# Reordering the start of a four-layer attention and MLP kernel on one Trainium2 core

## The chip, the cores and the metric

The kernel runs on one core of one Trainium2 chip. The metric is the device time of one execution in microseconds (us), and the number that counts is the median over runs. The engines are TensorE (PE in the profile, with its weight loads as PEld), VectorE (DVE), ScalarE (ACT), GpSimd (POOL) and SyncE (SP), which does nothing here but issue DMA transfers.

## The reference, cut to what matters

```python
x = A_x                                            # 1 x 2048 x 512, bf16
x = x + attention(layernorm(x), wqkv, w_phi, wo)   # layer 0
x = x + mlp(layernorm(x), W_gate, W_up, W_down)    # layer 1
x = x + attention(layernorm(x), ...)               # layer 2, the same weights
x = x + mlp(layernorm(x), ...)                     # layer 3, the same weights

def attention(x):                                  # 32 heads of 16
    q, k, v = split(x @ wqkv)
    phi(u) = concat(softmax(u @ w_phi), softmax(-u @ w_phi))
    kv = phi(k).T @ v                              # sums over all 2048 rows
    z = phi(k).sum(rows)
    return (phi(q) @ kv) / (phi(q) @ z + 1e-6) @ wo

def mlp(x):
    return (relu(x @ W_gate) * (x @ W_up)) @ W_down    # 512 -> 1376 -> 512
```

## The kernel before

The 2048 rows are 16 tiles `t` of 128 rows, which lie in `x_sb` from the start to the end. Every step of the whole program is recorded as an operation with an engine, a function, the data that it reads and writes, and two guessed costs in nanoseconds (`ii`, the time its engine is held; `lat`, the time until its result is there). A list scheduler (`Program.schedule`) then plays the program through eight times with these guesses and with a guess for DMA (`DMA_ISSUE`, `DMA_FIXED`, `DMA_BW`), and keeps the best order. So each engine runs a fixed order of instructions, and each instruction waits for semaphores of what it reads. A changed guess or priority can change the order on any engine.

What the first 55 us do:

- **Constants on VectorE.** `rowi` is a row 0..31, made by doubling (L446, L449); a 32x32 transpose (L450) gives `coli`, `colf` (L452) is its first column as f32, and four comparisons (L456) give the identity `ident`. From it come `m8` (L458) and `mask2` (L459). GpSimd clears small buffers (`vones` L463, `hr0` L465) and copies the mask (`kvsm` L466).
- **The folded key weights.** The 16x16 maps `w_phi` are folded into the key and query weights. `wk0` to `wk3` (L494) are four blocks of the key weights. TensorE transposes each (`WkT mm`, L527), ACT or DVE copies the result out (`WkT cp`, L532 and L534), a product with the block diagonal `BD` (L518, from `w128` and `m8`) makes `Wkp` (`Wkp mm` L542, `Wkp cp` L546 and L548). No key tile can start before all four blocks of `Wkp` are there. The query weights take the same way, transposed by DMA (`wT`, L485).
- **The tiles.** For every tile `t`: statistics `stat` (L559) and `aggr` on DVE, the reciprocal deviation `ln` and `rstd` (L562, L564) on ACT, the normalized tile `y` on DVE (L579) or, for the tiles in `POOL_Y`, on GpSimd (`nmr` L574, `yp` L576). Its transpose `yT` is made by TensorE and ACT for tiles 0, 1 and 2 (L588, L591) and by a DMA transpose on SP (L594) for the others. Then TensorE makes the keys `K` (L612) and the values `V` (L635), four matmuls of 128x512 each; ACT takes the exponentials (L617), DVE sums and normalizes them (L618, L626), and `kv` (L671) sums over the tiles. The queries (L651) and the attention per tile follow.

All loads go over two queues. SP issues, in this order, `wk0`..`wk3`, the tiles `x2`-`x3`, `wv`, `x4`-`x7`, the four `wT`, `x8`-`x11`, `x12`-`x15`, then the transposes `yT0.3`, `yT0.4` and so on to `yT0.15` (the name is layer, then tile), then the weights of the later layers. ACT issues `x0`, `wphi` (the load of `w128`, in elements of 32 bytes) and `x1`. Five matmuls of 128x512 on zeros (`warm`, L514) run on TensorE before the first weights land.

Of the kernel before, what the change touches and what calls it, by code (L numbers as in the profile page):

```python
# [5 lines left out]
FP32 = mybir.dt.float32  # L6
BF16 = mybir.dt.bfloat16
ALU = mybir.AluOpType
ACT = mybir.ActivationFunctionType
AX = mybir.AxisListType  # L10
# [38 lines left out]

class Program:  # L50
    SYNC = 40.0
    DMA_ISSUE, DMA_FIXED, DMA_BW = 520.0, 1500.0, 230.0
    TR_ISSUE, TR_FIXED, TR_TIME = 1250.0, 1050.0, 250.0

    def __init__(self, n_dma_sems=64):
        self.ops = []
        self.n_dma_sems = n_dma_sems

    def op(self, eng, fn, reads=(), writes=(), parts=(), ii=100.0, lat=None, name="", claims=(), after=(), dma=None, nbytes=0):
# [37 lines left out]
        self.ops.append(o)  # L97
        return o


    def links(self):
        for o in self.ops:
# [26 lines left out]
    def forward(self, prio, look=60.0):  # L129
# [4 lines left out]
        for o in ops:  # L134
            o.npend = len(o.deps) + len(o.order)
            o.ready = 0.0
            o.prio = prio[o.i]
            for t in o.tiles:
                tiles[id(t)] = t
        for t in tiles.values():  # L140
            t.slot, t.before, t.left = None, (), len(t.users)
            t.pool.held = [None] * len(t.pool.slots)
        free = dict.fromkeys(ENGINES, 0.0)
        bus = 0.0
        ready = {e: [] for e in ENGINES}
        for o in ops:
# [231 lines left out]
def build_kernel(nc, A_x, A_wqkv, A_w_phi, A_wo, B_x, B_W_gate, B_W_up, B_W_down, out):  # L378
# [20 lines left out]
    BD = sb("BD", [NC, 128])  # L399
    w128 = sb("w128", [NC, 16])  # L400
    m8 = sb("m8", [8])
    rowi, coli, colf = sb("rowi", [32]), sb("coli", [32]), sb("colf", [1], FP32)
    ident = sb("ident", [128])
    mask2 = sb("mask2", [8])
    eps = sb("eps", [1], FP32)
# [35 lines left out]
    c_BD = [res("BD", a) for a in range(4)]  # L441
    c_row, c_col = res("row"), res("col")
    wm, c_warm = tile(p_ga, "warm")
    op("dve", lambda e: e.memset(wm.ap(), 0.0), writes=[c_warm], ii=150, lat=210, name="warm")
    op("dve", lambda e: e.memset(ident[:], 0.0), writes=[c_id], ii=60, lat=100, name="id0")
    op("dve", lambda e: e.memset(rowi[:, 0:1], 0.0), writes=[c_row], ii=30, lat=70, name="row0")  # L446
    for k in range(5):
        n = 1 << k
        op("dve", lambda e, n=n: e.tensor_scalar(rowi[:, n:2 * n], rowi[:, 0:n], float(n), None, ALU.add), reads=[c_row], writes=[c_row], ii=70, lat=150, name="row")  # L449
    op("dve", lambda e: e.transpose(coli[:], rowi[:]), reads=[c_row], writes=[c_col], ii=100, lat=215, name="col")  # L450
    c_colf = res("colf")
    op("dve", lambda e: e.tensor_copy(colf[:], coli[:, 0:1]), reads=[c_col], writes=[c_colf], ii=70, lat=150, name="colf")  # L452
    c_idq = [res("identq", q) for q in range(4)]
    for q in range(4):
        sl = slice(32 * q, 32 * q + 32)
        op("dve", lambda e, sl=sl: e.tensor_scalar(ident[sl, sl], rowi[sl, :], colf[sl, :], None, ALU.is_equal), reads=[c_row, c_colf, c_id], writes=[c_idq[q]], ii=75, lat=150, name="identq")  # L456
    c_id = c_idq
    op("dve", lambda e: e.tensor_reduce(m8[:], ident[:].rearrange("p (h d) -> p h d", d=16), AX.X, ALU.add), reads=c_id, writes=[c_m8], ii=200, lat=290, name="m8")  # L458
    op("dve", lambda e: e.tensor_reduce(mask2[:].rearrange("p (a b) -> p a b", b=2), ident[:].rearrange("p (a f b) -> p a b f", f=16, b=2), AX.X, ALU.add), reads=c_id, writes=[c_m2], ii=200, lat=290, name="mask2")  # L459
    op("dve", lambda e: e.memset(eps[:], 1e-5), writes=[c_eps], ii=35, lat=70, name="eps")  # L460
    va_all = p_va.slots
    for i in range(16):
        op("pool", lambda e, i=i: e.memset(va_all[i][:, :, 128:130], 1.0), writes=[res("va1", i)], ii=60, name="vones")  # L463
    for i in range(2):
        op("pool", lambda e, i=i: e.memset(p_hr.slots[i], 0.0), writes=[res("hr0", i)], ii=500, name="hr0")  # L465
    op("pool", lambda e: e.tensor_copy(kvs[:, :, 136:144], mask2[:].unsqueeze(1).to_broadcast([P, 8, 8])), reads=[c_m2], writes=[res("kvsm")], ii=200, lat=280, name="kvsm")  # L466


    xv = A_x.rearrange("b (t p) d -> p (b t) d", p=P)
    outv = out.rearrange("b (t p) d -> p (b t) d", p=P)  # L470
# [19 lines left out]
    for ic in range(4):  # L490
        t, r = tile(p_hT, "wkn", ic)
        wk_n.append((t, r))
    def load_wk(ic):
        load("sp", lambda e: e.dma_start(wk_n[ic][0].ap(), A_wqkv[ic * 128:(ic + 1) * 128, 512:1024]), [wk_n[ic][1]], 131072, f"wk{ic}")  # L494
    load_x("act", 0, 1)
    load_wk(0)
    load("act", lambda e: e.dma_start(w128[:], A_w_phi.rearrange("(c h) d f -> (h d) c f", c=4)), [c_w128], 16384, "wphi")
    load_wk(1)
    load_wk(2)
    load_x("act", 1, 2)  # L500
    load_wk(3)
    load_x("sp", 2, 4)
    c_wv, c_wo = res("wv"), res("wo")
    load("sp", lambda e: e.dma_start(wv[:], A_wqkv[:, 1024:1536].rearrange("(c p) f -> p c f", p=P)), [c_wv], 524288, "wv")
    load_x("sp", 4, 8)
    for ic in range(4):
        load_wT(t_wq, c_wqT, 0, ic)
    load_x("sp", 8, 12)
    load_x("sp", 12, 16)


    pt_w, r_w = tile(p_ps, "warm")
    for k in range(5):
        op("pe", lambda e: e.matmul(pt_w.ap(), wm.ap()[:, 0:128], wm.ap(), start=True, stop=True), reads=[c_warm], writes=[r_w], ii=430, lat=600, name="warm")  # L514


    for a in range(4):
        op("dve", lambda e, a=a: e.tensor_tensor(BD[:].rearrange("p c (a f b) -> p c a f b", f=16, b=2)[:, :, a], w128[:].unsqueeze(3).to_broadcast([P, 4, 16, 2]),  # L518
                                                 m8[:, 2 * a:2 * a + 2].unsqueeze(1).unsqueeze(1).to_broadcast([P, 4, 16, 2]), ALU.mult),
           reads=[c_w128, c_m8], writes=[c_BD[a]], ii=190, lat=280, name="BD")  # L520

    for ic in range(4):
        pt, pres = tile(p_ps, "WkT", ic)
# [32 lines left out]
    def ln(l, ts):  # L556
# [9 lines left out]
        for t in ts:  # L566
            s = t // 4
            if (l, s) not in yT:
                yT[l, s] = Tile(f"yT{l}.{s}", p_yT)
            dst = yT[l, s]  # L570
            rr = res("yT", l, t, tile=dst)
            yt, yr = tile(p_y, "y", l, t)
            if (l, t) in POOL_Y:
                op("pool", lambda e, t=t: e.tensor_scalar(nmr[:, t, :], mv[:, t, 0:1], rstd[:, t, :], -1.0, ALU.mult, ALU.mult), reads=[res("mv", t), res("rstd", t)], writes=[res("nmr", t)],  # L574
                   ii=100, lat=170, name=f"nmr{l}.{t}")
                op("pool", lambda e, t=t, yt=yt: e.tensor_scalar(yt.ap(), x_sb[:, t, :], rstd[:, t, :], nmr[:, t, :], ALU.mult, ALU.add), reads=[res("x", t), res("nmr", t), res("rstd", t)],  # L576
                   writes=[yr], claims=[dst], ii=1000, lat=1050, name=f"yp{l}.{t}")
            else:
              op("dve", lambda e, t=t, yt=yt: e.tensor_scalar(yt.ap(), x_sb[:, t, :], mv[:, t, 0:1], rstd[:, t, :], ALU.subtract, ALU.mult),  # L579
               reads=[res("x", t), res("mv", t), res("rstd", t)], writes=[yr], claims=[dst], ii=323, lat=405, name=f"y{l}.{t}")  # L580
            c = (t % 4) * 128
            if (l, t) in PE_Y:
                pt, pres = tile(p_ps, "yps", l, t)

                def mm(e, yt=yt, pt=pt):
                    b16 = pt.ap().bitcast(BF16)
                    for k in range(4):
                        i = e.transpose(b16[:, k * 128:(k + 1) * 128], yt.ap()[:, k * 128:(k + 1) * 128], ident[:])  # L588
                    return i
                op("pe", mm, reads=[yr] + c_id, writes=[pres], ii=230, lat=400, name=f"yT{l}.{t}")  # L590
                op("act", lambda e, pt=pt, dst=dst, c=c: e.activation(dst.ap()[:, :, c:c + 128], pt.ap().bitcast(BF16)[:, 0:512].rearrange("p (k n) -> p k n", k=4), ACT.Copy),  # L591
                   reads=[pres], writes=[rr], ii=477, lat=600, name=f"yTcp{l}.{t}")
            else:
                op("sp", lambda e, yt=yt, dst=dst, c=c: e.dma_start_transpose(dst.ap()[:, :, c:c + 128], yt.ap()), reads=[yr], writes=[rr],  # L594
                   dma="tr", nbytes=131072, name=f"yT{l}.{t}")
# [277 lines left out]
    for l in (0, 2):  # L873
        for s in range(NS):
            for c in range(4):
                q_chunk(l, s, c)
        kv_sums(l)
        for t in range(NT):
            attn_tile(l, t)
            ln(l + 1, [t])  # L880
        for s in range(NS):
            hv = [(0, 2), (2, 4)] if s == 0 else [(0, 4)]
            halves_of[l + 1, s] = hv
            glu_slab(l + 1, s, hv)
            for t in range(4 * s, 4 * s + 4):
                down(l + 1, t, last=(l == 2))
                if l == 0:
                    ln(2, [t])
                    kv_tile(2, t)
    pr.schedule(ROUNDS)  # L890
    pr.prepare()
    block = E(nc.Block())
# [15 lines left out]

ROUNDS = 8
ACT_RZ = {(0, t) for t in range(16)} | {(2, t) for t in range(0, 16, 2)}  # L910
POOL_Y = {(0, t) for t in range(4, 16)}
PE_Y = {(0, 0), (0, 1), (0, 2), (1, 0), (1, 1), (2, 15), (3, 0), (3, 1)}
PE_O = {(0, 0), (0, 1), (2, 0), (2, 1)}

# [42 lines left out]
```

## Time and profile before

| | |
|---|---|
| median of 8 runs | 398.33 us |
| lowest and highest run | 397.07 and 399.66 us |
| the profiled execution's own time | 398.31 us |
| its span, first to last instruction | 396.5 us |
| TensorE busy | 380.3 us, 96% of the span |
| VectorE, ScalarE, GpSimd busy | 71%, 50%, 11% |
| mean granted TensorE clock | 0.994 |

The span leaves out 1.8 us of the measured time that lie around the instructions. "L612" is line 612 of the kernel before. In a timeline row the first number is the start in us, the second the time that the row's instructions took together, `x4` their count, and the bracket the idle time of the engine before them with what ended it.

### The profile page before, as it was taken

How to read it: one execution, taken by the hardware profiler on the slowest of the kernel's cores; microseconds unless marked ns; L12 is line 12 of the kernel's file. 1: busy time of each engine (PE TensorE's matmuls, PEld its weight loads, DVE VectorE, ACT ScalarE, POOL GpSimd, SP SyncE). 2: the span in 40 equal slices, each digit the busy share in tenths (PEclk: the TensorE clock that was granted, in tenths of full speed). 3: DMA queues.
4: the chain of work that ended last, by engine and by line, in shares of the span. 5: the costliest groups of instructions: out<-in, count | busy, mean ns of one | idle time of the engine just before them, and what ended most of it. 6: DMA issues, size and time to landing. Idle time of an engine off the chain costs nothing.

```text
span 396.5 us, 6502 instructions
## 1 busy us (share of the span) xinstructions
PE 380.3 (96%) x2362; PEld 209.6 (53%) x2405; DVE 283.5 (71%) x599; ACT 199.7 (50%) x615; POOL 43.4 (11%) x143
## 2 busy tenths in 40 slices
PE   6879999899999999999999999989999999999996
PEld 3434755677655444444444466567765544444442
DVE  8969957998889636536699993799888962433424
ACT  4969779765444304303149966976544430303300
POOL 2371012221111000000000001222111100000000
PEclk9989999999999999999999999999999999999999
DMA  8846900134231402002022000014423140110012
GB/s 224 176 94 154 354 30 8 34 76 85 45 63 28 80 15 40 14 2 40 13 43 52 2 2 2 13 32 78 80 50 61 26 79 15 40 37 17 0 48 73
DMA packets 63439, 23.02 MB, mean 58 GB/s; under 512 B 54352, under 2 KB 63408, under 8 KB 63408
## 3 DMA queue, kind: packets, MB, share of 16 engines
q1 hardware_dynamic: 62592, 22.33, 24.7%
q8 instruction: 19, 0.31, 0.3%
q10 hardware_dynamic: 816, 0.28, 0.3%
q14 instruction: 12, 0.10, 0.1%
HBM read 7.91 MB, written 2.10 MB: 25 GB/s over the span
## 4 chain that ended last, share of the span: by engine, by line
PE 74%; ACT 12%; DVE 8%; DMA 2%; POOL 2%; issue 1%; SPq 0%
PE pb L794 30%; PE pb L846 17%; PE pb L635 6%; ACT expq L655 5%; PE pb L612 4%; PE pb L764 4%; PE pb L671 4%; ACT phik L617 3%; PE pb L651 2%; PE pb L822 2%; PE pb L848 2%; PE pb L704 2%; DVE t L738 1%; DVE stats L559 1%; DVE hT L802 1%; ACT sm L718 1%
## 5 line engine op out<-in xcount | busy, mean ns | idle before, releaser
L801 ACT ACTIVATE gate<-pb 128x512 bf16<-128x512 f32 (+1 forms) x100 | 50.7, 509 | 101.3 <-PE pb L794 100.5
L794 PE MATMUL pb<-yT,Wg 128*128 128x512 bf16 (+1 forms) x395 | 83.0, 336 | 0.3
L794 PE MATMUL pb<-yT,Wu 128*128 128x512 bf16 (+1 forms) x393 | 82.5, 336 | 0.4
L802 DVE TENSOR_TENSOR hT<-gate,pb 128x512 bf16<-128x512 bf16 (+1 forms) x100 | 56.4, 576 | 35.6 <-PE pb L794 35.2
L846 PE MATMUL pb<-Wd,hT 128*128 128x512 bf16 x310 | 73.6, 379 | 0.4
L794 PEld LDWEIGHTS pb<-yT,Wg 128*128 128x128 bf16 x400 | 37.7, 98 | 32.9 <-DVE hT L802 1.5
L794 PEld LDWEIGHTS pb<-yT,Wu 128*128 128x128 bf16 x400 | 38.4, 98 | 28.0 <-DVE hT L802 0.5
L846 PEld LDWEIGHTS pb<-Wd,hT 128*128 128x128 bf16 x320 | 31.2, 98 | 37.9
L852 DVE TENSOR_TENSOR x_sb<-x_sb,pb 128x512 bf16<-128x512 bf16 x32 | 21.8, 682 | 37.3 <-PE pb L848 37.3
L559 DVE BATCH_NORM_STATS2 stats<-x_sb 128x6 f32<-128x512 bf16 x64 | 43.1, 685 | 0.4
L618 DVE TENSOR_REDUCE z<-phik 128x64 f32<-128x1024 bf16 x32 | 37.5, 1208 | 3.7 <-ACT rz L623 3.7
L655 ACT ACTIVATE expq<-pb 128x512 bf16<-128x512 f32 x64 | 35.0, 608 | 8.7 <-PE pb L651 8.7
L738 DVE TENSOR_TENSOR t<-pb,sm 128x384 bf16<-128x384 f32 x64 | 32.6, 549 | 7.6 <-POOL sm L729 6.8
L617 ACT ACTIVATE phik<-pb 128x512 bf16<-128x512 f32 x64 | 35.6, 641 | 4.6 <-PE pb L612 4.5
L562 ACT ACTIVATE lnv<-mv,eps 128x1 f32<-128x1 f32 (+2 forms) x56 | 16.4, 298 | 41.4 <-DVE mv L560 41.3
L725 POOL TENSOR_TENSOR sm<-sm 128x64 f32<-128x64 f32 x32 | 10.5, 327 | 228.3 <-ACT sm L718 228.3
L612 PE MATMUL pb<-Wkp,yT 128*128 128x512 bf16 x124 | 30.8, 391 | 2.7 <-DMA yT<-y 2.5
L767 DVE TENSOR_TENSOR x_sb<-x_sb,pb 128x512 bf16<-128x512 bf16 x32 | 21.7, 679 | 14.2 <-PE pb L764 14.2
L764 PE MATMUL pb<-wo,oT 128*128 128x512 bf16 x120 | 30.5, 379 | 0.7
L651 PE MATMUL pb<-yT,Wqp 128*128 128x512 bf16 x122 | 29.7, 380 | 1.3 <-DVE t L738 0.8
L635 PE MATMUL pb<-wv,yT 128*128 128x512 bf16 x125 | 30.2, 383 | 0.2
L579 DVE TENSOR_SCALAR y<-x_sb,mv,rstd 128x512 bf16<-128x512 bf16 x52 | 21.1, 409 | 3.3 <-ACT rstd L564 3.3
(69 smaller groups left out, 384.8 us busy)
## 6 DMA issues: line engine op xcount, KB each, us to landing
out_dram<-x_sb SPq DMA_DIRECT2D x16, 128.0 KB, 1.7
x_sb<-in_A_x_dram SPq DMA_DIRECT2D x3, 512.0 KB, 5.3
Wg<-in_B_W_gate_dram SPq DMA_DIRECT2D x2, 640.0 KB, 7.9
Wu<-in_B_W_up_dram SPq DMA_DIRECT2D x2, 640.0 KB, 9.1
Wd<-in_B_W_down_dram SPq DMA_DIRECT2D x1, 1280.0 KB, 13.3
yT<-y SPq DMA_TRANSPOSE x56, 2.5
hT<-in_A_wqkv_dram SPq DMA_DIRECT2D x4, 128.0 KB, 3.8
wv<-in_A_wqkv_dram SPq DMA_DIRECT2D x1, 512.0 KB, 6.2
```

Of the source, the lines that this page charges most:

```text
L559: op("dve", lambda e, t=t: e.bn_stats(stats[:, t, :], x_sb[:, t, :]), reads=[res("x", t)], writes=[res("st", t)], ii=600, lat=690, name=f" ...
L612: i = e.matmul(kt.ap(), src.ap()[:, ic, c0:c0 + 128], Wkp[:, ic, :], start=(ic == 0), stop=(ic == 3))
L617: op("act", lambda e, s=s: e.activation(ft.ap()[:, s, :], kt.ap(), ACT.Exp, scale=(1.0, -1.0)[s]), reads=[kr], writes=[fr2[s]], ii=477, la ...
L618: op("dve", lambda e: e.tensor_reduce(zt.ap().rearrange("p (a b) -> p a b", b=2), ft.ap().rearrange("p s (a f b) -> p (s a) b f", f=16, b= ...
L635: i = e.matmul(vt.ap(), src.ap()[:, ic, c0:c0 + 128], wv[:, ic, :], start=(ic == 0), stop=(ic == 3))
L651: i = e.matmul(qt.ap(), Wqp[:, ic, c * 128:(c + 1) * 128], src.ap()[:, ic, :], start=(ic == 0), stop=(ic == 3))
L655: op("act", lambda e, g=g: e.activation(es[g][0].ap(), qt.ap(), ACT.Exp, scale=(1.0, -1.0)[g]), reads=[qr], writes=[es[g][1]], ii=477, lat ...
L764: i = e.matmul(wt.ap(), oT_.ap()[:, c, :], wo[:, c, :], start=(c == 0), stop=(c == 3))
L794: i = e.matmul(pt.ap()[:, 0:n], W[:, ic, fc * 128:(fc + 1) * 128], src.ap()[:, ic, a * 128:b * 128], start=(ic == 0), stop=(ic == 3))
L801: op("act", lambda e: e.activation(st_.ap()[:, 0:n], gt.ap()[:, 0:n], ACT.Relu), reads=[gr], writes=[sr], ii=110 + n * .72, lat=230 + n * ...
L802: op("dve", lambda e: e.tensor_tensor(ht.ap()[:, a * 128:b * 128], st_.ap()[:, 0:n], ut.ap()[:, 0:n], ALU.mult), reads=[sr, ur], writes=[h ...
L846: i = e.matmul(pt.ap(), hT[l, s, fc].ap()[:, c:c + 128], Wd[:, fc, :], start=(fc == 0), stop=False)
```

## The change

The change touches the first microseconds and the guesses that order them:

- `warm`: 40 matmuls of 128x128 take the place of 5 of 128x512. The scheduler may place them between others.
- The identity: `rowi` by eight memsets and two additions; the comparison is between `rowi` and `coli` directly, and `colf` is gone.
- `BD`: two of its four parts go from DVE to GpSimd. The small GpSimd operations are told to come after them.
- Loads: `x0` and `x1` go from ACT's queue to SP's, `wk0` from SP's to ACT's behind `wphi`; `x4`-`x7` is split in two; `x1` comes after `wk3`.
- The tiles 4 and 5 of layer 0 leave `POOL_Y`: DVE makes their `y`.
- A new method `first` adds to the priority of all that the keys of tiles 0 to 3 need; and several guesses of the scheduler change.

In the built program the order of the instructions differs from the one before in the first 50 us; behind that it is the same on every engine. On SP the transposes now come as `yT0.3`, `yT0.6`, `yT0.7`, `yT0.4`, `yT0.5`, `yT0.8` and so on, and TensorE takes the tiles as 0, 1, 2, 3, 6, 7, 4, 5, 8. The four `Wqp mm` still stand between `K0.0` and `K0.3`. On GpSimd, the first arithmetic is now `BD`; ahead of it stands a configuration instruction (ISA) that stood ahead of `nmr` before.

```diff
-    DMA_ISSUE, DMA_FIXED, DMA_BW = 520.0, 1500.0, 230.0
+    DMA_ISSUE, DMA_FIXED, DMA_BW = 470.0, 1600.0, 270.0
+    def first(self, goals, step):
+        for k, g in enumerate(goals):
+            stack = [g.i]
+            while stack:
+                i = stack.pop()
+                if i not in self.boost:
+                    self.boost[i] = (len(goals) - k) * step
+                    stack += self.ops[i].deps + self.ops[i].order
-            o.prio = prio[o.i]
+            o.prio = prio[o.i] + self.boost.get(o.i, 0.0)
-        free = dict.fromkeys(ENGINES, 0.0)
+        free = dict.fromkeys(ENGINES, 750.0)
...
-    for k in range(5):
-        n = 1 << k
-        op("dve", lambda e, n=n: e.tensor_scalar(rowi[:, n:2 * n], rowi[:, 0:n], float(n), None, ALU.add), ...)
+    for k in range(8):
+        op("dve", lambda e, k=k: e.memset(rowi[:, k:k + 1], float(k)), parts=[c_row], ...)
+    op("dve", lambda e: e.tensor_scalar(rowi[:, 8:16], rowi[:, 0:8], 8.0, None, ALU.add), ...)
+    op("dve", lambda e: e.tensor_scalar(rowi[:, 16:32], rowi[:, 0:16], 16.0, None, ALU.add), ...)
-    op("dve", lambda e: e.tensor_copy(colf[:], coli[:, 0:1]), ...)
-        op("dve", lambda e, sl=sl: e.tensor_scalar(ident[sl, sl], rowi[sl, :], colf[sl, :], None, ALU.is_equal), ...)
+        op("dve", lambda e, sl=sl: e.tensor_tensor(ident[sl, sl], rowi[sl, :], coli[sl, :], ALU.is_equal), ...)
...
-    load_x("act", 0, 1)
-    load_wk(0)
-    load("act", ... [c_w128], 16384, "wphi")
+    load_x("sp", 0, 1)
+    load("act", ... [c_w128], 65536, "wphi")
+    load_wk(0, "act")
     load_wk(1)
     load_wk(2)
-    load_x("act", 1, 2)
     load_wk(3)
+    load_x("sp", 1, 2)
     load_x("sp", 2, 4)
...
-    load_x("sp", 4, 8)
+    load_x("sp", 4, 6)
+    load_x("sp", 6, 8)
...
-    for k in range(5):
-        op("pe", lambda e: e.matmul(pt_w.ap(), wm.ap()[:, 0:128], wm.ap(), ...), ii=430, lat=600, name="warm")
+    for k in range(WARM):
+        op("pe", lambda e: e.matmul(pt_w.ap()[:, 0:128], wm.ap()[:, 0:128], wm.ap()[:, 0:128], ...), ii=107 if k < 30 else 56, lat=300, name="warm")
...
-        op("dve", lambda e, a=a: e.tensor_tensor(BD[:]...), ii=190, lat=280, name="BD")
+        o_bd = op("pool" if a % 2 else "dve", lambda e, a=a: e.tensor_tensor(BD[:]...), ii=290 if a % 2 else 190, lat=340 if a % 2 else 280, name="BD")
+    # vones, hr0 and kvsm moved here, each with after=[o_bd]
...
-                   ii=100, lat=170, name=f"nmr{l}.{t}")
+                   ii=233, lat=260, name=f"nmr{l}.{t}")
-                   writes=[yr], claims=[dst], ii=1000, lat=1050, name=f"yp{l}.{t}")
+                   writes=[yr], claims=[dst], ii=742, lat=762, name=f"yp{l}.{t}")
+    pr.first([kop[0, t] for t in range(FIRST)], 1e5)
-POOL_Y = {(0, t) for t in range(4, 16)}
+POOL_Y = {(0, t) for t in range(6, 16)}
+WARM = 40
+FIRST = 4
```

## The prediction

> **What bounds the kernel now.** I read the page first, its slices above all, then the busy times by stage, then TensorE's timeline at the one hole, then SP's timeline and GpSimd's instructions. Of the 40 slices (9.9 us each) TensorE has its weakest at the start and in the third, 19.8 to 29.7 us, where the granted clock dips too; behind that it is full to the end:
>
> ```profile
> PE   6879999899999999999999999989999999999996
> PEclk9989999999999999999999999999999999999999
> ```
>
> The busy times of the first 55 us, cut where TensorE stops and starts (columns: stretch, its length, busy time and count for each engine, clock, DMA share, GB/s):
>
> ```profile
> 0.00:9.50 9.50, 6.12 (x37) 3.75 (x37) 7.88 (x30) 4.08 (x8) 2.00 (x23) 1.00 0.88 228
> 9.50:17.69 8.19, 7.04 (x52) 3.93 (x53) 8.19 (x21) 7.35 (x23) 1.29 (x4) 1.00 0.89 202
> 17.69:19.60 1.91, 1.90 (x8) 0.69 (x8) 1.91 (x7) 1.91 (x7) 1.91 (x5) 1.00 0.79 73
> 19.60:21.88 2.28, 0.00 (x0) 0.00 (x1) 2.28 (x9) 1.55 (x5) 1.24 (x4) 1.00 0.37 55
> 21.88:26.60 4.72, 4.67 (x14) 1.81 (x16) 3.75 (x4) 2.49 (x6) 3.50 (x6) 0.64 0.46 91
> 26.60:55.10 28.50, 28.34 (x224) 16.91 (x226) 24.04 (x31) 24.85 (x71) 3.96 (x8) 1.00 0.69 199
> ```
>
> From K0.3 at 17.69 to the second slab's queries at 55.10, 37.41 us, TensorE either works or stands in one hole of 2.28 us, and after the hole it works 4.72 us at a mean clock of 0.64, which loses 0.36 x 4.72 = 1.70 us. The work itself is 37.41 - 2.28 - 1.70 = 33.43 us. So the stage ends at (start of K0.3) + 33.43 + holes + lost clock, and an earlier first key helps only if K0.3 also comes earlier. What each of these starts waits for is in TensorE's and SP's timelines:
>
> ```profile
> 16.47 1.06 PE L542 MATMUL pb<-BD,yT 128*128 128x128 bf16 x16
> 17.69 1.04 PE L612 MATMUL pb<-Wkp,yT 128*128 128x512 bf16 x4 [0.16 <-DMA yT<-y]
> 18.56 1.03 PE L635 MATMUL pb<-wv,yT 128*128 128x512 bf16 x4
> 21.88 1.04 PE L612 MATMUL pb<-Wkp,yT 128*128 128x512 bf16 x3 [2.29 <-DMA yT<-y]
> ...
> 24.03 3.17 PE L612 MATMUL pb<-Wkp,yT 128*128 128x512 bf16 x8
> ```
>
> ```profile
> 4.14 6.72 SPq L485 DMA_TRANSPOSE yT<-in_A_wqkv_dram  x4
> 10.90 1.13 SPq L479 DMA_DIRECT2D x_sb<-in_A_x_dram  x2
> 12.08 22.37 SPq L594 DMA_TRANSPOSE yT<-y  x13
> ```
>
> yT0.3 is issued at 12.08 behind 1 MB of x, and lands just before 17.69: that is the queue, not the data. The hole is yT0.4; the chain of waits says why it is late:
>
> ```profile
> 16.90 0.77 POOL y L576 x2
> 17.67 4.17 DMA yT<-y
> 21.88 0.60 PE pb L612 x2
> ```
>
> GpSimd writes y0.4 only at 17.6, and its transpose takes 4.17 us where the 56 of the page take 2.5 in the median.
>
> **The change part by part.** The sum is made on the profiled execution, 398.31 us (span 396.5 and 1.8 around it); the median, 398.33, is the same.
>
> *Warm-up, identity, load order, priority.* In the identity, rowi's eight memsets cost 8 x 0.04 (the spacing of the rows at 0.81 and 0.85), two additions 0.17 each, the transpose 0.21, the four comparisons 0.25 each: with gaps the mask reduction starts at about 2.9 instead of 4.23. Nothing follows: the first transposes then wait for weights. wk0 now sits behind wphi on ACT's queue; all four wk, x0 and wphi are as many bytes as before, and the chain before has the third wk landing at 6.37. I put the last of the four at 6.4, between 5.9 (issue 2.1 plus the page's median of 3.8) and 6.9. Then 0.62 (four transposes, L527), 0.60 (copy), 0.40 (four products, L542), 0.66 (cast, L548) and four gaps of 0.05 give K0.0 at 8.9, where it is 12.14 now. Up to K0.3 TensorE has six groups of 0.86 (5.2), the 16 Wqp products (1.06) and two transposes of y (0.4 together), and I add 0.5 for waits on ACT and DVE: free for K0.3 at 16.1. The 40 matmuls themselves are cover: 26 at 0.107 (the 0.43 of a 128x512 one, a quarter) end at 4.3, before the weights; nine behind the last Wkp product lie beside the cast of 0.66, and at half clock would add 0.3, hidden too. So three microseconds are won, and **all of them are swallowed by the wait for yT0.3**.
>
> *yT0.3.* It still stands behind x8 and x12, and those behind the four wT. SP gains three issues (x0, x1, the second half of x4-x7) and loses one (wk0): 2 x 0.46 (1.82 us for four) = 0.9 later. But the four wT issues took 6.72 us, against 4 x 1.32 later on (5.27 for four at 29.18): 1.4 us of SP standing still there, which can take the 0.9. Besides, a 16 KB instruction packet falls on one DMA engine at 18 to 21 us (queue q8 in the DMA table, 19 over the run for 4800 TensorE instructions); it lies in yT0.4's 4.17. With 35 more matmuls it comes some 70 instructions earlier, into the loads of x8 and x12, for 0 to 1.7 (4.17 - 2.5). Bounds for K0.3: 0.3 earlier (no byte is removed, only the gaps can close) to 2.6 later; I take 0.5 later, near the end at which SP's standstill covers the issues, so 18.2.
>
> *The hole.* The order is now 0.3, 0.6, 0.7, 0.4, 0.5. y0.6 needs its statistics (now 14.75 for the fourth of that batch on DVE), ln and rstd (0.33, 0.25), which now stand on ACT right behind K0.1's exponentials, with no copy of V between them, then 0.49 and 0.76 on GpSimd: about 16.5 (15.9 to 17.6), lands 2.5 later at 19.0. TensorE needs it at 18.2 + 1.73 = 19.9: no hole. y0.4 is on DVE behind the statistics of tiles 8 to 14 (the old order has the thirteenth at 18.8), done at about 20.3, lands 23.0; TensorE needs it at 19.9 + 3.45 = 23.4. Close, so I charge 0.3 for both, with bounds 0 and 1.7 (one more stretched transpose). The 2.28 goes.
>
> *The clock.* The 1.70 goes with the hole, unless the new wait before K0.3, 18.2 - 16.1 = 2.1 us, does the same: at most 1.7, at least 0. I take a third, 0.5, since the wait can also be shorter (1.0 with K0.3 at 17.7 and a TensorE free at 16.7). The rows have a drop after 2.28 us without a matmul. The Trainium skill, "TensorE: Matmul & The Clock Gate", in its table "Why this matters for your kernels", asks for idle gaps under about 3 us and names one full idle window as what throttles; by it 2.1 us cost nothing and the gain would be 0.5 larger. This trace contradicts it with 2.28 us, and the trace decides.
>
> *GpSimd's BD.* Rows of 128x32 at 0.25 and 128x64 at 0.33 give 0.48 for 128 elements, 0.95 for two, against 0.28 each on DVE; done at 5.2, before the last weights: covered. The first Wkp product waits for it, and behind that on TensorE the fourth WkT transpose and yT0.0. The small GpSimd operations come after BD now, at 5 to 7 us; DVE's additions took 0.58 and 0.45 instead of 0.17 while GpSimd cleared hr0, so a copy or y0.0 on DVE can lose 0 to 0.8 there, under yT0.3's wait too. The trace has one more thing here: the configuration instruction runs at 4.95, and the first arithmetic starts at 16.40, 0.09 after the rstd that it waited for. Whatever the instruction sets off lay under 11.4 us of idleness and now stands before BD: 0 to 11.4 us. I take 0, as no traffic but loads, transposes and instruction fetches shows in the DMA table then. The skill's "GPSIMD Engine Reference", section 2.1, gives about 6 us for the first call after such a load, without a visible instruction; by it BD would be done at 7.7 instead of 5.2, K0.0 about 0.3 later, still under yT0.3's wait. No run here shows which holds.
>
> *VectorE.* It takes y0.4 and y0.5 (0.32 each), gives two BD (0.2 each), plus 0.25. From 26.6 on it idles 28.50 - 24.04 = 4.46: it caps the gain at 4.2 and doesn't bind below.
>
> Sum: 2.28 + 1.70 - 0.5 - 0.3 - 0.5 = 2.7 us; 398.3 - 2.7 = **395.6**. After 50 us the order is the same on every engine, and the loads of the MLP weights, issued from 34.5 (13.3 for the slowest), are first used past 75: the shift is kept.
>
> **The rivals.**
> - *The transposes come later and the hole only moves.* yT0.3 is 1.5 to 2.6 late, by SP's issues and the fetch, and the wait drops the clock: 3.98 - 1.5 - 0.3 - 1.7 gives 0.5, with 2.6 it is -0.6: 397.8 to 398.9. For it: both waits and the fetch are there; against it: 1.4 us of slack on SP. Chance 0.20.
> - *GpSimd's configuration holds BD, slower.* K0.0 comes 1.5 after BD (product, cast, gaps), K0.3 7.2 later, and the clock, idle meanwhile, costs 1.7: K0.3's time is (end of the hold) + 0.95 + 1.5 + 7.2 + 1.7. It equals the old stage's 55.10 - 33.43 = 21.67 for a hold until 10.3, so it decides from 9.5 us of hold on; at the bound, until 12.2, it costs 1.9: 400.2. Against it: nothing in the trace asks for that long. Chance 0.12.
> - *VectorE binds*: a gain of 4.2 and no more, 394.1; this is the low end of my own case.
>
> **How the numbers follow.** My case has 0.68, from 394.0 (nothing late, 0.3 won) to 397.0 (0.9 late and the clock dropped: 3.98 - 0.9 - 1.7 = 1.4). Range 394.0 to 398.6: the first rival lies nearly whole in it, the second outside. This kernel's measurement tells 0.3% from no change, 1.2 us. Faster: 0.66 of my case and 0.06 of the first rival, 0.72. Same: 0.16, the rest of the first rival and the mild part of the second. Slower: 0.12.
>
> **What would show it.** Right: K0.0 at 8.5 to 9.5; K0.3 at 17.7 to 18.7 with an idle time before it put down to DMA yT<-y; no hole over 1 us behind it; clock 1.00 from 20 to 30; the second slab's queries at about 52.4. Wrong: K0.0 after 11 with Wkp waiting for POOL BD (second rival); K0.3 after 19.5 or a clock of 0.5 in 18 to 25 (first); or queries at 52.4 and yet no gain, if later transposes are stretched.

## The result: slower by 0.4%, and the profile after

| | before | after |
|---|---|---|
| median | 398.11 us (57 runs) | 399.48 us (20 runs) |
| lowest and highest | 395.55 and 400.86 | 395.99 and 402.27 |
| profiled execution, its span | 398.31, 396.5 | 399.65, 397.9 |
| mean granted clock in it | 0.994 | 0.999 |

The ratio is 1.0037 with a 95% interval of 1.002 to 1.0054. The prediction was 395.6, faster. So a gain of 2.7 us was forecast and a loss of 1.4 came, and both have to be found. The ratios, and the 19 executions of after that are counted below, leave out those more than 1.5% above the fastest of the same kernel.

The first key tile came as forecast. The 40 slices of after show no dip of the clock, but TensorE's dip in the third slice has only moved to the second, and a new one stands in the eighth:

```profile
PE   7699999799999999999999999989999999999996
PEclk9999999999999999999999999999999999999999
```

The busy times by stage, cut where TensorE stops and starts (stretch, length, then each engine's busy time and count, the clock, the DMA share and GB/s):

```profile
8.30:17.60 9.30, 6.98 (x47) 3.53 (x48) 6.44 (x17) 6.88 (x21) 1.48 (x4) 1.00 1.31 211
17.60:20.00 2.40, 0.01 (x1) 0.01 (x1) 2.40 (x5) 1.77 (x6) 0.51 (x1) 1.00 1.19 165
20.00:25.00 5.00, 4.95 (x23) 2.27 (x25) 5.00 (x16) 3.78 (x10) 0.74 (x3) 1.00 0.38 75
```

K0.0 starts at 8.53 (12.14 before). But TensorE then stands still from 17.6 to 20.0, as long as it stood from 19.6 to 21.9 before. Its timeline names the wait, one tile earlier than before:

```profile
16.99 0.61 PE L555 MATMUL pb<-BD,yT 128*128 128x128 bf16 x8
19.99 1.04 PE L625 MATMUL pb<-Wkp,yT 128*128 128x512 bf16 x3 [2.39 <-DMA yT<-y]
```

SP's timeline and the chain of waits show why yT0.3 is late:

```profile
5.12 7.11 SPq L489 DMA_TRANSPOSE yT<-in_A_wqkv_dram  x4
12.28 2.21 SPq L483 DMA_DIRECT2D x_sb<-in_A_x_dram  x2
14.53 21.38 SPq L607 DMA_TRANSPOSE yT<-y  x13
```

```profile
14.53 5.42 DMA yT<-y
19.95 0.05 issue
19.99 0.61 PE pb L625 x2
```

It is issued at 14.53 instead of 12.08: x8 goes out 1.38 later, and the two issues of x8 and x12 hold SP for 2.21 instead of 1.13. From issue to landing it needs the same as before (5.42 and 5.56).

The second slab's queries come 0.82 us earlier than before; so much is won there. They are lost again in two stops at the out-projections (wo), layer 0 tile 3 and layer 2 tile 15; the timelines of both stretches:

```profile
72.22 0.48 PE L717 MATMUL pb<-kvs,expq 128*128 128x144 bf16 x5
74.38 0.81 PE L777 MATMUL pb<-wo,oT 128*128 128x512 bf16 x3 [1.68 <-ACT lnv L575]
```

```profile
322.01 1.04 PE L777 MATMUL pb<-wo,oT 128*128 128x512 bf16 x4 [0.79 <-DMA oT<-o]
```

ScalarE is the wrong suspect in the first one. The view of the tile oT from 69 to 76 us shows two transposes, one of which took 4.2 us (it landed at 74.11, 0.04 before the weight load), and the DMA table of 71 to 73 us shows what else ran then:

```profile
DMA to landing us min/median/max: 2.4/3.3/4.2
```

```profile
q8 instruction: 1, 0.02, 3.6%
```

Queue q8 carries TensorE's own instructions, 16 KB a packet, 19 in the run, one for about every 125 matmuls. In the trace's packet records this one starts at 71.88. Relative to before, after falls back by 1.53 us at the first stop and by 1.15 at the second (packet at 319.11); 0.5 of it is regained in between. Neither is in the profile of before, whose packets fall elsewhere.

Two more profiles of after and one of before were taken later; they make the balance less dependent on one execution. Measured from the first profile of before:

| | second slab's queries | last matmul |
|---|---|---|
| before, two profiles | 0, +0.10 | 0, +0.53 |
| after, three profiles | -0.82, -1.28, -0.25 | +1.34, +2.62, +0.94 |

On average after is 0.83 us ahead at 55 us and loses 2.20 behind that; 1.37 is also the difference of the medians. The experiments ask where the start's 2.7 went, and where the 2.2 come from.

### The profile page after: what moved, and what is told of

Read it like the earlier page. It is cut to its first block, busy times and chain, and to the rows that moved or that the text cites. A ratio compares the mean times of both kernels' runs of the same rounds, so it can differ in the third digit from the quotient of the medians.

```text
span 397.9 us, 6572 instructions
## 1 busy us (share of the span) xinstructions
PE 379.0 (95%) x2397; PEld 210.6 (53%) x2440; DVE 282.8 (71%) x602; ACT 200.0 (50%) x615; POOL 43.4 (11%) x141
## 4 chain that ended last, share of the span: by engine, by line
PE 66%; ACT 13%; DVE 10%; DMA 5%; POOL 2%; issue 2%; SPq 1%; ACTq 0%; POOLq 0%
PE pb L807 30%; PE pb L859 16%; ACT expq L668 5%; PE pb L648 4%; PE pb L777 3%; ACT phik L630 3%; PE pb L684 2%; DMA yT<-y 2%; PE pb L664 2%; PE pb L835 2%; PE pb L625 2%; PE pb L861 2%; DMA x_sb<-in_A_x_dram 2%; DVE stats L572 2%; DVE t L751 2%
## 5 line engine op out<-in xcount | busy, mean ns | idle before, releaser
L592 DVE TENSOR_SCALAR y<-x_sb,mv,rstd 128x512 bf16<-128x512 bf16 x54 | 22.2, 414 | 3.5 <-ACT rstd L577 3.5
```

## The experiments

Three theories. **Theory 1**: the change adds 35 matmuls to the warm-up, so every instruction packet of TensorE comes 35 matmuls earlier, and a DMA transpose that it meets lands 1 to 2 us late. **Theory 2**: the load edits (x0 and x1 on SP's queue, wk0 on ScalarE's, x4 to x7 in two) make yT0.3 late. **Theory 3**: the wait before K0.3 costs the granted clock. In all kernels below the scheduler's order of after (or before) is kept; only the named instructions change, and "..." in an edit marks lines left out. Each was timed beside the kernel before, except where one profile was enough.

### The number of matmuls, without any change of order

Fewer of them in after: ten wide ones in place of 40 narrow ones.

```diff
-        op("pe", lambda e: e.matmul(pt_w.ap()[:, 0:128], wm.ap()[:, 0:128], wm.ap()[:, 0:128], ...), ...)
+        o_w = op("pe", lambda e: e.matmul(pt_w.ap(), wm.ap()[:, 0:128], wm.ap(), ...), ...)
+        if k % 4: pr.drop.add(o_w.i)
...
```

The lines left out skip the dropped operations when the program is built and clear all 512 columns of `wm`.

> The kernel after, with its 40 warm-up matmuls of 128x128 issued as ten of 128x512 at the same places, so that TensorE runs 30 matmuls (60 instructions) fewer; every other instruction of every engine keeps its place. Theory 1 (the places of TensorE's instruction packets decide; the packets come about every 125 matmuls): each packet comes 30 matmuls later. The first, at 13.05 us after, comes near 19.9; x8 and x12 are no longer behind it, and K0.3 starts at 18.9 (18.0 to 19.3) instead of 19.99. The packets of 71.88 and 319.11 us come at about 76.7 and 325.5, where the trace of after has no transpose 0.6 to 2.25 us old: the stops of 1.7 and 0.8 us at the out-projections (wo) go. Total 395 to 397, ratio to before 0.992 to 0.997. Theory 2 (the loads' order and queue make yT0.3 late, and the rest is chance): K0.3 stays at 19.9 to 20.1, total as after, 399.5, ratio 1.003 to 1.004.

Measured: ratio 1.0016 (0.9992 to 1.0041). Both stops are gone, but K0.3 stays at 20.07, as theory 2 said, and two other transposes are hit: the first packet came at 26.54 and not at 19.9, on yT0.8 (4.16 us, with a wait of 1.79 before K0.8), and one at 122.95 on the oT of tile 13:

```profile
125.46 1.02 PE L781 MATMUL pb<-wo,oT 128*128 128x512 bf16 x4 [1.04 <-DMA oT<-o]
```

So theory 1 holds for the stops and not for the late start. The count fixes the first packet's place only roughly: here it comes 29 matmuls later than counted, and in the two profiles of before (the second follows below) it comes at 18.74 and at 25.98.

More of them in after:

```diff
-                for c in range(4):
+                for c in [0, 1, 2] + [3] * (1 + (PAD if name == "Wqp" and ic == 3 else 0)):
...
+PAD = 24
```

> The kernel after, with 24 repeats of the last matmul of the fourth Wqp product, which write the same values again; they stand in the 2.4 us in which TensorE waits for yT0.3 anyway (24 x 0.06 = 1.4 us). No other instruction changes. Theory 1 (places of the instruction packets): the start up to K0.3 is as after, 20.0; from the second packet on each comes 24 matmuls earlier. The one of 71.88 falls at 67.3, 0.3 us after the issue of an oT transpose, and the 1.7 us stop at the out-projection goes; the ones of 97.4, 115.9, 135.9, 281.4, 295.8 and 314.1 now fall 0.8 to 2.2 us behind an issue. So the traces differ at just these places and the total moves, by up to 3 us to either side: I expect 397.5, 396 to 400. Theory 2: the total stays at 399.5 within 0.3.

Measured: 397.38, ratio 0.9982 (0.9957 to 1.0006). Neither stop is in its profile: at the end it is as far from before as at 55 us (0.42 and 0.39 later, after a half-clock stretch behind K0.3). K0.3 at 19.8.

The same number in before:

```diff
+    def warm(e):
+        for j in range(8):
+            i = e.matmul(pt_w.ap()[0:32, 0:64], wm.ap()[:, 0:32], wm.ap()[:, 0:64], start=True, stop=True)
+        return i
-        op("pe", lambda e: e.matmul(pt_w.ap(), wm.ap()[:, 0:128], wm.ap(), start=True, stop=True), ...)
+        op("pe", warm, ...)
```

> The kernel before, with each of its five warm-up matmuls of 128x512 issued as eight of 128x64 with 32 weight columns, so 35 matmuls more, as many as after has; nothing else changes, on no engine. Theory 1: the packets come 35 matmuls earlier. The first, at 18.74 us before, comes near 13.4, 1.3 us after the issue of yT0.3, and no longer stretches yT0.4 to 4.17 us: the hole of 2.28 us before K0.4 shrinks to that of GpSimd alone, about 0.6, or K0.3 itself comes up to 1.5 later. Later packets fall on other transposes (99.4, 122.2, 164.5, 267.6, 301.0, 322.2). Total between 396 and 401, different from before's by more than 0.7 us. Theory 2 (the count of matmuls is nothing, the order is all): total 398.1, hole of 2.28 as before.

Measured: ratio 1.001 (0.9985 to 1.0035); the sum is unmoved, against my expectation, but its parts are not. In TensorE's timeline the hole of 2.28 us before K0.4 is gone, K0.3 waits 1.38, and the stop of after at wo, tile 3, is there in a kernel that has nothing of the change but the count:

```profile
18.61 1.04 PE L617 MATMUL pb<-Wkp,yT 128*128 128x512 bf16 x4 [1.38 <-DMA yT<-y]
...
71.77 0.81 PE L769 MATMUL pb<-wo,oT 128*128 128x512 bf16 x3 [1.46 <-DMA oT<-o]
```

The hole that the change was to remove was made by a packet too: with the packet elsewhere yT0.4 took 2.44 instead of 4.17. At 55 us this kernel is 3.2 us ahead of the profile of before; it loses 1.34 at wo tile 3 and 1.13 at the last wo. The rows of the first product behind the second slab's queries, of before and of this kernel:

```profile
56.01 1.16 PE L704 MATMUL pb<-kvs,expq 128*128 128x144 bf16 x16
52.78 1.16 PE L709 MATMUL pb<-kvs,expq 128*128 128x144 bf16 x16
```

Issue-to-landing times of three oT transposes, over all profiles, by the matmuls that stand ahead of them more than in before:

| matmuls more | kernels | oT0.3 | oT0.13 | oT2.15 |
|---|---|---|---|---|
| 0 | before, twice | 2.4 | 2.4 | 2.5 |
| 5 | ten wide warm-ups, loads new or old | 2.8, 2.5 | **4.2, 4.1** | 2.5 |
| 17 | ten wide warm-ups and twelve repeats, four kernels | 2.5 to 2.7 | 2.4 | 2.5 to 2.6 |
| 35 | after three times, before with 35 more, old loads | **4.0 to 4.3**, once 3.1 | 2.4 | **3.9 to 4.1** |
| 35 | the filled wait (below), twice | 2.9, 2.8 | 2.4 | **3.6, 4.1** |
| 59 | 24 repeats | 2.9 | 2.4 | 2.6 |

The same count hits the same transposes in kernels with different starts. oT0.3 lies at the edge: it is hit in four of the seven profiles with 35 more, and the 3.1 of the third profile of after stopped nothing there. The rule also holds without counting. In all 16 profiles together, from 60 us on, a TensorE packet starts 0.5 to 2.1 us after the issue of 63 transposes of `y` or `o`, and these took 3.05 to 4.52 us; the 765 with no packet of 8 or 16 KB from 1.5 us before their issue to 3 us after it took 2.39 to 2.56. That settles theory 1 for the later loss. The Trainium skill, "Runtime: NRT & Kernel Launch", section "Instruction fetch mechanics", calls the cost of crossing a 16 KiB block mostly hidden. For TensorE itself the traces agree: no idle time over 0.7 us behind the tenth us is put down to anything but data. But they show a price of 0.6 to 2.1 us for transposes in flight, of which that sentence says nothing.

### The loads

After with the loads of before:

```diff
...
+    new = [ld[n] for n in ("x0", "wk0", "wphi", "wk1", "wk2", "x1", "wk3", "x2", "wv", "x4", "x6")]
+    for n, eng in (("x0", "act"), ("x1", "act"), ("wk0", "sp")): ld[n].eng = eng
+    pr.alias[ld["x6"].i] = ld["x4"]
+    ld["x4"].fn = lambda e: e.dma_start(x_sb[:, 4:8, :], xv[:, 4:8, :])
+    pr.sequence = new + [o for o in pr.sequence if o not in new]
```

> The kernel after with the loads as before: x0 and x1 on ScalarE's queue around wphi, wk0 first on SyncE's, x4 to x7 in one load; all other instructions in the order of after, so the same count of matmuls. Theory 2 (order and queue of the loads make yT0.3 late): x8 is issued at 10.9 to 11.5 instead of 12.28, yT0.3 lands at 17.7 to 18.5, K0.3 starts at 17.8 to 18.6 and the total falls by 1.4 to 2.2, to 397.5; K0.0 comes later, at 8.5 to 9.5. Theory 1 (the first packet at 13.05 on the wT transposes makes them late): yT0.3 lands at 19 to 20 as after, total 398.9 to 399.5.

Measured: ratio 1.0027 (0.9999 to 1.0054). The SP times of theory 2 came true (x8 issued at 10.33, yT0.3 at 12.14), and K0.3 did not move. The chain of waits:

```profile
12.14 7.77 DMA yT<-y
19.91 0.05 issue
19.96 1.03 PE pb L628 x2
```

Issued 2.4 us earlier than in after, yT0.3 takes 7.77 instead of 5.42. The packet records have TensorE's packet at 14.79 (0.98 us) and one of another engine's at 15.31 that took 3.36 us, both while yT0.3 is under way. Over the 16 profiles yT0.3 took 4.95 to 6.22 us where no TensorE packet starts during it (seven profiles), and where one does (nine) 6.7 to 8.0 in seven and 5.2 and 5.4 in two. So here a packet may have taken the place of the late loads. Both undoings together:

> The kernel after with both of the earlier single undoings together: the loads as before, and the warm-up as ten matmuls of 128x512 (30 matmuls fewer). [...] Theory 1 and 2 together: K0.3 at 17.5 to 18.2, clock full in at least 10 of 12 executions, no stop at wo0.3 and wo2.15, but the stop of 1.8 us at K0.8 and of 1.2 at wo0.13 as in the other kernel with ten warm-up matmuls; 395.7 (395 to 397). If neither is the cause of the late yT0.3: K0.3 at 20.0, 397.8.

Measured: 396.59, ratio 0.9968 (0.9945 to 0.999); K0.3 at 17.27, a wait of 1.15 before K0.8, and the stop at wo tile 13, 1.13 us, as foretold. With twelve repeats (`PAD = 12` in the diff of the 24) to move the packets off both:

> As the kernel with both undoings, and twelve repeats of the last matmul of the fourth Wqp product (0.06 us each), which bring every later instruction packet of TensorE twelve matmuls forward. Theory 1: the stop at K0.8 (packet at 26.5 on yT0.8) moves to another transpose or goes, as do those at wo0.13 (packet at 123 on an oT transpose) and wo2.7 to wo2.9; the profile differs from the one without the repeats at these places. K0.3 at 17.7 to 18.4; 395 (393.8 to 397). Without theory 1: as the one without repeats, up to 0.5 later.

Measured: **394.93, ratio 0.9919 (0.9893 to 0.9946)**, and six of its eight executions lie within 0.11 us of the median (the others took 395.14 and 400.86). This beats both kernels. Its chain of waits and TensorE's slices:

```profile
12.18 5.19 DMA yT<-y
17.37 0.05 issue
17.41 0.61 PE pb L633 x2
```

```profile
PE   7999999999999999999999999999999999999996
```

The second slab's queries come 3.33 us before those of before and the last matmul 3.38: nothing is lost behind them. The slices show no weak one after the first. But the first product behind the queries comes only 0.11 us earlier than the 52.78 of the kernel before with 35 matmuls more, which has nothing else of the change:

```profile
52.67 1.16 PE L725 MATMUL pb<-kvs,expq 128*128 128x144 bf16 x16
```

So by these profiles nearly all that the fastest kernel wins up to the queries can come from where the packets fall. What the rest of the change adds is not shown: no run has the kernel before with its packets off both stops. Without its stops of 1.34 and 1.13 the kernel before with 35 more would take about 395.1, an estimate from its profiled 397.58.

Which load edit? The split of x4 to x7 put back alone, and the queues alone, both from the fastest kernel:

```diff
-    pr.alias[ld["x6"].i] = ld["x4"]
-    ld["x4"].fn = lambda e: e.dma_start(x_sb[:, 4:8, :], xv[:, 4:8, :])
```

> The kernel with the loads as before, ten warm-up matmuls and twelve repeats, with one part of the new loads put back: x4 to x7 in two loads of 256 KB instead of one of 512. Theory 2a (one more issue on SyncE and nothing else): the wT transposes, x8, x12 and yT0.3 are issued 0.46 later, K0.3 at 17.8 to 18.1 instead of 17.41, total 395.0 to 395.6. Theory 2b (the split itself makes the loads slower from 6 to 9 us, where the new loads carry 200 to 300 KB per us against 320 to 370): K0.3 at 19 to 20, total 396 to 398.

```diff
-    new = [ld[n] for n in ("x0", "wk0", "wphi", "wk1", "wk2", "x1", "wk3", "x2", "wv", "x4", "x6")]
-    for n, eng in (("x0", "act"), ("x1", "act"), ("wk0", "sp")): ld[n].eng = eng
+    new = [ld[n] for n in ("x0", "wphi", "wk1", "wk0", "wk2", "wk3", "x1", "x2", "wv", "x4", "x6")]
```

> As the fastest kernel so far (loads as before, ten warm-up matmuls of 128x512, twelve repeats: K0.3 at 17.41, 394.93 us), with the other part of the new loads put back: x0 and x1 on SyncE's queue, wk0 on ScalarE's behind wphi; x4 to x7 stay one load. The split alone gave K0.3 at 18.85 and 395.6. If the queues make the loads slower: at 8 us 1400 to 1500 KB have arrived instead of 1749, K0.3 at 19 to 20, 396.5 to 398. If only the number of issues counts: K0.3 at 17.8 to 18.9, 395 to 396.

Measured for the split: 395.59, ratio 0.9959 (0.9932 to 0.9986), K0.3 at 18.85; for the queues: 399.66, ratio 1.0031 (1.0005 to 1.0058), K0.3 at 18.64. The busy times of 4 to 9 us (GB/s last), of after and of the fastest kernel:

```profile
4.00:9.00 5.00, 4.07 (x57) 3.41 (x55) 4.34 (x12) 3.54 (x9) 1.91 (x20) 1.00 0.95 256
```

```profile
4.00:9.00 5.00, 4.42 (x41) 2.96 (x39) 4.28 (x10) 3.05 (x7) 2.58 (x21) 1.00 1.11 330
```

Before has 318 GB/s there, the split 310, the queues alone 273. Over all profiles, the seven with the old queues have 302 to 330 GB/s there and the nine with the new ones 232 to 289. So it is the move of x0, x1 and wk0 that slows the loads, and by the two ratios the move costs some 4.5 us. Its profiled execution does not show all of this: it took 396.28, with no wait of over 1 us before K0.3, while seven of its twelve executions have a mean clock under 0.997. Last, all new loads, with the packets of the fastest kernel:

> The kernel after with all its load edits, ten warm-up matmuls of 128x512 instead of 40 of 128x128, and twelve repeats of the last matmul of the fourth Wqp product: TensorE's instruction packets lie as in the fastest kernel. Theory 2 (the load edits cost the start): K0.3 at 19.5 to 20.1, 2 to 2.6 later than in the fastest kernel, no stop at wo0.3, wo0.13 and wo2.15, total 397 to 397.6 where the clock stays full, 1.5 more in executions where the wait before K0.3 lowers it. If the loads cost nothing once the packets are moved: 395.

Measured: 399.55, ratio 1.0017 (0.9991 to 1.0043). The stops are gone as expected; the price was set too low. K0.3 came 3.5 us late instead of 2 to 2.6, and eight of twelve executions are under 0.997. The first packet (17.78 us, 2.05 long) started while yT0.3 was under way (7.96 us from issue to landing); that it is the cause is not shown, since in the queues-only kernel one at 17.96 (0.95 long) left yT0.3 at 5.39. TensorE's timeline:

```profile
21.12 0.92 PE L629 MATMUL pb<-Wkp,yT 128*128 128x512 bf16 x3 [3.55 <-DMA yT<-y]
```

The two-by-two table of medians:

| | 40 warm-up matmuls | ten wide ones and twelve repeats |
|---|---|---|
| new loads | 399.48, ratio 1.0037 (after) | 399.55, ratio 1.0017 |
| old loads | 398.77, ratio 1.0027 | **394.93, ratio 0.9919** |

Each undoing alone moves the ratio by 0.001 to 0.002, less than its interval is wide, and both move it by 0.012. They meet in one deadline: yT0.3 must land before TensorE runs out of work at about 17.4.

### The clock

In the timed executions the mean granted clock is under 0.997 in 11 of 19 of after (the 11 take 400.2 on average, the others 398.3), and in 5 of 98 of before. The profile of before happens to be one with a half-clock stretch.

Fill the wait (and, to keep the count, issue the first twelve warm-up matmuls as three wide ones):

```diff
...
+                for k in range(9 if name == "Wqp" and ic == 3 else 0):
+                    e.matmul(pt.ap(), srcT.ap()[:, 0, 0:128], BD[:].rearrange("p c n -> p (c n)"), start=True, stop=True)
```

> The kernel after with its wait before K0.3 filled: nine matmuls of 128x512 ahead of the fourth Wqp product, into the same PSUM tile, which the product then overwrites (9 x 0.216 = 1.9 us of the 2.4), and, to keep the count of matmuls, the first twelve warm-up matmuls as three of 128x512. So TensorE's instruction packets stay where they are in after from the fourth Wqp product on. Theory 3 (the wait of 2.4 us before K0.3 lowers the granted clock in many executions; in after 11 of 19 executions have a mean clock of 0.994 to 0.996 and a mean time of 400.2, the 8 others 398.3): with the wait filled the clock stays full in at least 10 of 12, and the mean falls to 398.3. Theory 1 (instruction packets) keeps its two stops: at wo0.3 (1.3 to 1.7 us later relative to the profile of before) and at wo2.15 (1.0 to 1.2). If the clock falls elsewhere or for another reason: as after, 399.4, half of the executions at 0.994 to 0.996.

Measured: 401.52, ratio 1.0071 (1.0034 to 1.0107), six of nine under 0.997: my expectation was wrong. So profiles of more executions:

> The kernel with nine 512-wide matmuls in the wait before K0.3 once more. Its timed executions refuted my expectation: 6 of 9 have a mean clock of 0.994 to 0.996 and take 402.1 us, 3.5 more than the others, while its profile (full clock) has K0.3 at 19.69 after 1.26 us of waiting. Theory 3 in its remaining form: in the slow ones yT0.3 lands later still, so that a wait of 2 us or more is left, K0.3 comes at 21 or later and the half clock follows it. Otherwise the half clock follows another wait.

Measured: full clock again, 399.76; K0.3 at 20.90 after 1.56 us of waiting, yT0.3 7.48 us from issue to landing. Changing the first twelve warm-ups had moved the first packet from 13.05 to 14.7 and 15.2, closer to yT0.3, so this kernel changed more than the wait. It stays inconclusive.

> The kernel after once more, for a profile of an execution with the lower mean clock (11 of its 19 timed executions have 0.994 to 0.996). Theory 3 (the wait before K0.3 costs the clock): in such an execution the half clock stands right behind K0.3, for 3 to 5 us, and the wait before it is 2.2 us or more. If the clock falls elsewhere: half clock at another place, behind another wait.

> The same again, since not every execution shows the lower clock: half clock right behind the wait before K0.3 (theory 3), or elsewhere.

Both have the lower clock. In the second, TensorE's timeline and the busy times show it right behind the wait for yT0.3: four matmuls take 1.89 instead of 1.04.

```profile
15.93 0.61 PE L555 MATMUL pb<-BD,yT 128*128 128x128 bf16 x8
18.94 1.89 PE L625 MATMUL pb<-Wkp,yT 128*128 128x512 bf16 x4 [2.40 <-DMA yT<-y]
20.62 1.86 PE L648 MATMUL pb<-wv,yT 128*128 128x512 bf16 x4
22.32 1.03 PE L625 MATMUL pb<-Wkp,yT 128*128 128x512 bf16 x4
```

```profile
18.90:22.30 3.40, 3.36 (x8) 1.19 (x9) 3.40 (x15) 1.08 (x2) 0.00 (x0) 0.50 0.27 53
```

In the first it stands elsewhere, behind the stop at wo tile 3 that the packet makes, and there the stop costs 3.1 us instead of 1.5:

```profile
73.76 1.89 PE L777 MATMUL pb<-wo,oT 128*128 128x512 bf16 x4 [1.51 <-ACT sm L740]
```

```profile
73.70:77.00 3.30, 3.24 (x13) 1.71 (x14) 1.42 (x4) 0.86 (x5) 0.32 (x1) 0.53 0.20 40
```

A half clock that begins within 1.2 us of the end of a wait for yT0.3 is in three more profiles: the 24 repeats (row: 2.17), the old loads (3.37) and the last kernel of the loads (row: 3.55); in the first and the last of these the record of the first matmul is missing, so that the wait is 0.2 shorter than its row. So theory 3 is half right: the wait before K0.3 costs the clock in some executions, and the stop at wo tile 3 can do the same. The waits before the drops are 2.40 and 1.51 us (the latter with 0.80 of idleness shortly before), and the waits of 2.39 and 2.40 before K0.3 in the first two profiles of after and of 2.24 with ten wide warm-ups have none right behind them. The Trainium skill, "TensorE: Matmul & The Clock Gate", section "What's actually happening", says that the window is free-running, not tied to the kernel's start; that fits equal waits with unequal outcomes. Its bound of about 3 us in the table that the prediction weighed is not what these rows show.

Before once more:

> The kernel before once more, for a second profile of it. In the timed executions its mean clock is 0.998 to 1.000 in 34 of 35, while its profile has 0.994. Theory 3: the profile shows the full clock; the hole of about 2.3 us before K0.4 is there (the instruction packet at 18.7 stretches yT0.4), but without the half clock behind it, so that the second slab's queries come 1.4 to 1.8 us earlier than 55.1; other places then lose what keeps the time at 397 to 398.5.

Measured: 398.84, full granted clock, queries 0.10 later than in the first profile. My expectation of 1.4 to 1.8 earlier failed: the 2.28 before K0.4 were 0.53 here, but TensorE's pace at the start was half until 15 us, which the clock column does not report:

```profile
10.94 1.91 PE L635 MATMUL pb<-wv,yT 128*128 128x512 bf16 x4
12.64 1.91 PE L612 MATMUL pb<-Wkp,yT 128*128 128x512 bf16 x4
```

K0.3 came at 19.78, and the packet at 25.98 made a hole of 1.30 farther on. The start of before loses about as much in both profiles, in different places.

## Why the prediction was wrong, step by step

- **K0.0 at 8.9: right.** 8.53, and up to 9.4 in the other kernels with the new start. So was GpSimd's `BD`: the row of its two instructions has 0.90 us, where 0.95 was worked out, and ahead of them only the wait for w128. The second rival needed a hold until 9.5:

```profile
3.36 0.90 POOL L524 TENSOR_TENSOR BD<-w,m 128x128 bf16<-128x128 bf16 x2 [2.92 <-DMA w<-in_A_w_phi_dram]
```

  The 6 us that the Trainium skill, "GPSIMD Engine Reference", section 2.1, gives for such a first call are not seen.
- **yT0.3 later by 0.5: the first term that failed.** It landed 2.3, 1.8 and 1.3 later in the three profiles, inside the bounds of -0.3 to 2.6 but in their upper part. There are two errors in the term. I let SP's 1.4 us of standing still cover the issues, and charged the queue move nothing; the loads of 4 to 9 us ran at 256 to 266 instead of 318 GB/s, and x8 was issued 0.3 to 1.4 later. And I had bounded the packet with 0 to 1.7 and then left it out: in all three it starts during SP's two issues of x8 and x12, which take 2.21 there and 1.13 in the 13 other profiles, where it starts elsewhere.
- **The hole goes, 2.28: right where it stood, and answered by a wait of 2.39** one tile earlier. The prediction had this wait, at 2.1, and thought it free because TensorE came early; it was free only against a K0.3 at 18.2. Behind it, after needs 35.20 us from K0.3 to the first product behind the queries, 0.86 more than before without its hole and its half clock (38.32 - 3.98), where 0.3 was charged for waits. And the prediction closed the hole by the new order of the tiles; the kernel before with 35 matmuls more loses it too, with the old order.
- **The clock, 1.70 gone, 0.5 charged: wrong in its base.** The profile of before had a half-clock stretch that 93 of 98 timed executions do not have, so 1.70 was no part of the median that was to be beaten. That the profile and the median agree in their sum (398.31 and 398.33) said nothing of their parts. After, the drop came in 11 of 19, for 1.9 us each.
- **"The shift is kept" after 50 us: the second step that failed.** By the average of the profiles it cost 2.2 us. I argued from an unchanged order. The order was unchanged and the count was not: in the first profile 1.53 and 1.15 us went at two transposes that the packets now meet. In the second a half-clock stretch follows the first stop, in the third the first stop is missing. The prediction had named this ("no gain, if later transposes are stretched") and given it no price.
- **The rivals.** "The transposes come later and the hole only moves" was the right mechanism for the start (K0.3 1.5 to 2.6 late; 397.8 to 398.9); with the two later stops the time lies above it. VectorE did not bind: the fastest kernel gains 3.4 us by the profiles, under the cap of 4.2.
- **The mechanism was right in part.** With old loads and packets elsewhere K0.3 starts at 17.41, the queries at 51.8 (52.4 foretold) and the kernel takes 394.93, 3.2 us under before by the ratio. But the kernel before with 35 matmuls more comes to 0.11 us of it at the queries, with K0.3 at 18.61. So it is not shown how much of the 3.2 is due to the change's constants, priority and order, and how much to packets that meet no transpose with a deadline. Against the fastest kernel, after's loads and its 40 warm-up matmuls together cost some 4.6 us.

Open: what the change is worth with equal luck of the packets; what sets the place of the first packet; why x0, x1 and wk0 on the other queues slow the loads; where the clock falls in the executions of the queues-only kernel and of the filled one, of which no profile shows it; and which DMA engine a packet uses, since the records don't name it.

## What to carry to other kernels

When an edit adds or removes instructions, look where the instruction packets of the busiest engine will fall, and which transfers with a deadline are in flight there: a harmless filler can move a stall of 1 to 2 us to the far end of the kernel. Take two or three profiles of the kernel before, since a stretch of lower clock or a stretched transfer in one of them may be rare, and compare the clock of all executions. When two single undoings do nothing, try both together before dropping either: two causes of one late transfer can hide each other. And before crediting a gain to a new order, give the old kernel the same luck with its packets.

## What was not expected of the hardware

- One 16 KB instruction packet of TensorE (0.9 to 2.1 us, about every 125 matmuls) makes a DMA transpose in flight land late: 3.05 to 4.52 us in the 63 cases where it starts 0.5 to 2.1 us after the issue, instead of 2.39 to 2.56. One of 8 KB took 3.36 us in the midst of the loads.
- Moving three loads of 128 KB between the two queues, and nothing else, changed the rate of all loads from 330 to 273 GB/s over 5 us.
- The granted clock fell right behind a wait of 2.40 us in one execution and not behind 2.39 and 2.40 in two others of the same kernel, and the half clock then lasts 3.4 us.
